# Attention into a gated mixture of experts: four steps' rows turned on VectorE instead of TensorE, two small products put later, and weight quarters asked for earlier

## The chip, the cores and the metric

One core of a Trainium2 chip runs the whole kernel in one launch. The metric is the device time of an execution in microseconds (us). Three runs of the kernel before gave 443.42, 445.30 and 445.82 us; the median is 445.3.

The core's engines are named as the profile names them: PE (TensorE matmuls) with PEld (its weight loads), DVE (VectorE), ACT (ScalarE), POOL (GpSimd) and SP (SyncE, which here only issues DMAs). Each engine takes its instructions in order, and each waits by semaphores for the others and for DMAs.

## What is computed

A linear attention with decay, block by block, whose output is the input of a mixture of experts. Each token goes to one of eight experts: the one with the largest logit, or, where a local gate says so, the expert of the token before.

```python
# attention: B=4, H=8, S=768, D=64; per head a decay lam and a state kv (D x D)
intra = (q_blk @ k_blk.T * Dmask) @ v_blk
inter = (q_blk * lam_pow) @ kv_state
out[block] = intra + inter
kv_state = lam_block * kv_state + (k_blk * rev_pow).T @ v_blk
# x = out of all heads, (4, 768, 512); E=8 experts, F=1024
logits = x @ w_gate
local_gate = sigmoid(x @ w_local)
e = argmax(logits[s]) if s == 0 or local_gate[s] < 0.5 else e_of_token_before
y[s] = softmax(logits[s])[e] * (relu(x[s] @ w1[e]) @ w2[e])
```

## The kernel before

**Two stages.** The attention runs in 24 steps. Step `s` handles one chunk of 128 tokens of one of the four sequences (`ORDER`: six chunks, four sequences each; `b = s % 4`, chunk `c = s // 4`). The experts' stage follows: tiles of 128 tokens that belong to one expert are gathered from `x_dram` by row numbers and go through that expert's two weight matrices. Its first tile is expert 0's, then more tiles with one expert each, then pairs of tiles and smaller parts. Each of PE, DVE, SP and POOL works in the order in which the program is written (`manual_schedule`); only ACT's order is the scheduler's.

**One step `s` of the attention**, in program order (the loop at the end of the step functions below):

- SP asks for the input of step `s+5` (`loaded`, 1 MB, 0.75 MB from step 20 on) into one of six buffers, which step `s-1` must have left.
- POOL scales query and key of step `s+3` (`prepare`: `qd` L178, `kd` L181).
- In the steps in `QUARTERS`, SP asks for a quarter (512 KB) of the first expert's `w1` into `w1t[0]` (L831).
- PE makes the scores of step `s+1` (`scores`, tile `ps`); DVE multiplies them with the mask (`sm`, L213, two instructions). For the steps in `WIDE`, the scores are eight products of whole 128x128 blocks (L201); for the others they are sixteen smaller ones that leave out a quarter of each block that the mask makes zero (L209).
- PE multiplies the state with `qd` (`from_state`, L236); ACT decays the state (L240).
- `logits`, then the extra work listed for `(s, 0)`, then every fourth step `gates` (L308).
- PE mixes values (`mix`, L249) and ACT copies the result to `xc` (L252), which holds one chunk per sequence and so is written again four steps later.
- PE makes the state's addition (`update`, L263), DVE adds it (`kv`, L266).
- The 128 rows of step `s-1` have to be turned (features to rows) and written to `x_dram`. There are two ways. `rows_of` does it with four PE products into `pk` (L273), an ACT copy to `xn` (L278) and a 256 KB write on ACT's queue (L282). `turned_rows` does it with one DVE instruction (L294), for the steps in `TURNED`, which says in which step it is done; the four steps of a chunk share one half of `w1t[1]` as their buffer, and after the last of them `group_out` writes all four with four DMAs of 256 KB on SP's queue (L302).
- The extra work listed for `(s, 1)`.

**The extra work** finds each token's expert while the attention still runs: `fresh_experts` (DVE only, ends with `mark` L425), `along_sequences` (PE products of the marks L433, then DVE `stay` L436 and a scan `run` L442), `experts_of` (PE products of the runs L449, then DVE `hot` L451), `ranks` (PE L460 and L461 on `hot`, ACT, DVE), `masks` (`lane`, L485), `first_tiles`, `tokens_to_first_tiles`, `brought`, `by_slots`, `chances`. The index 0 stands for chunks 0 and 1, index 1 for chunk 2. In step 20, `ahead` makes POOL gather the rows of the first two tiles (L725, `xg<-x_dram`); `prepare` of step 22 stands ahead of it in POOL's order, and `prepare` of step 23 behind it.

**The hand-over.** In step 23 PE turns the first gathered tile (`first_turned`, L734), DVE copies it (`xt`, L735), and the first expert's first product follows (`hidden`, L753). `w2` of the first expert is asked for in step 20 (L833), the second expert's weights in step 23 (L836, L837).

**Semaphores of the DMAs.** The DMAs of SP's and ACT's queues take eight semaphores in turn, in the order in which the scheduler places them; a DMA that takes a semaphore waits until the one that had it before has landed, and SP issues nothing else in the meantime.

Of the kernel before, what the change touches and what calls it, by code (L numbers as in the profile page):

```python
# [24 lines left out]
B, H, S, DH = 4, 8, 768, 64  # L25
# [12 lines left out]
NA = B * CA  # L38
PARTS = [(0, 8), (8, NA), (NA, NT)]
LOADS = 6  # L40
QUARTERS = [16, 17, 18, 19]
WIDE = [3, 4, 5, 7, 9, 11]
TURNED = {**{r: r + 1 for r in range(3 * B)}, 11: 13, 20: 22, 21: 23, 22: 23}
WARM = 10
KA = -(-(NA * P - E * (P - 1)) // P)

# [19 lines left out]
def kernel(  # L66
# [106 lines left out]
    def prepare(s):  # L173
        b, c = ORDER[s]
        x = inp[s]
        if c:
            qd = qds[s] = att.tile([P, A, P], F32, name="qd", bufs=3)
            nc.gpsimd.tensor_tensor(qd, x[:, 0].rearrange("p (a i) -> p a i", i=P), lamq, ALU.mult)  # L178
        if c + 1 < NC:
            kd = kds[s] = att.tile([P, DM], F32, name="kd", bufs=3)  # L180
            nc.gpsimd.tensor_tensor(kd.rearrange("p (h d) -> p h d", d=DH),  # L181
                                    x[:, 3].rearrange("p (h d) -> p h d", d=DH),
                                    rev.unsqueeze(2).broadcast_to([P, H, DH]), ALU.mult)
# [3 lines left out]
    def scores(s):  # L187
# [8 lines left out]

        if s in WIDE:
            for a in range(A):
                for u in range(2):
                    rows = slice(DH * u, DH * u + DH)  # L200
                    nc.tensor.matmul(ps[u][:, a], lhsT=kt[rows, a], rhs=qt[rows, a],  # L201
                                     start=True, stop=True, skip_group_check=True)
        for a in range(A if s not in WIDE else 0):
            for j in range(2):
# [92 lines left out]
    def group_out(k):  # L297

        n = sum(r // B == k for r in TURNED)
        rows = x_dram[B * P * k:B * P * k + n * P, :]  # L300
# [72 lines left out]
    def constants_6():  # L373
        for k in range(4):
            nc.scalar.copy(dupq[:, QP * k:QP * k + QP], ident[:, :QP])
        row = ints[0][:, 2 * P:2 * P + 1]
        nc.vector.tensor_scalar(row, row, P - QP, None, ALU.bitwise_and)
        nc.vector.tensor_scalar(fourth, row, 1.0 / QP, None, ALU.mult)
# [19 lines left out]
    def pool(i):  # L398
        return pools[i == 2]

    def hot_of(i):
        lo, hi = PARTS[i]
        return hots[lo // NA][:, :, lo % NA:lo % NA + hi - lo]

    def fresh_experts(i):

        lo, hi = PARTS[i]
        n = hi - lo
        lg = lt[:, lo:hi, :E]
        if not i:  # L410
            nc.vector.memset(lt[0:1, :B, E:], -1.0)
        if i == 2:
            room = rt.tile([P, 2, NA, E], F32, name="each0", bufs=1).rearrange("p k n e -> p (k n e)")
            mx, best, mark = (room[:, n * (E + k):n * (E + k) + n] for k in range(3))
            top, mark = room[:, :n * E].rearrange("p (n e) -> p n e", e=E), mark.bitcast(BF16)[:, :n]
        else:
            mx, best = (rt.tile([P, n], F32, name=f"{k}{i}", bufs=1) for k in ("mx", "best"))
            top = rt.tile([P, n, E], F32, name=f"top{i}", bufs=1)
            mark = rt.tile([P, n], BF16, name=f"mark{i}", bufs=1)
        nows["mx", i], nows["mark"] = mx, mark  # L420
        nc.vector.tensor_reduce(mx, lg, axis=AX.X, op=ALU.max)
        nc.vector.tensor_tensor(top, lg, mx.unsqueeze(2).broadcast_to([P, n, E]), ALU.is_equal)
        nc.vector.tensor_tensor(top, top, down.unsqueeze(1).broadcast_to([P, n, E]), ALU.mult)
        nc.vector.tensor_reduce(best, top, axis=AX.X, op=ALU.max)
        nc.vector.scalar_tensor_tensor(mark, lt[:, lo:hi, E], FRESH, best, ALU.is_le, ALU.mult)  # L425

    def along_sequences(i):

        lo, hi = PARTS[i]
        n = (hi - lo) // B  # L430
        prow = pr[:B, :P * n]
        for c in range(n):
            nc.tensor.matmul(prow[:, P * c:P * c + P], lhsT=nows["mark"][:, B * c:B * c + B], rhs=identb,  # L433
                             start=True, stop=True, skip_group_check=True)
        stay = pool(i).tile([B, P * n], BF16, name=f"stay{i}", bufs=1)
        nc.vector.tensor_scalar(stay, prow, 0.0, None, ALU.is_equal)  # L436
        run = runs[i] = pool(i).tile([B, P * n], BF16, name=f"run{i}", bufs=1)
        before = 0.0
        if i:
            before = rt.tile([B, 1], F32, name="carry", bufs=1)  # L440
            nc.scalar.copy(before, runs[i - 1][:, -1:])
        nc.vector.tensor_tensor_scan(run, stay, prow, before, ALU.mult, ALU.add)  # L442

    def experts_of(i):
        lo, hi = PARTS[i]
        n = hi - lo
        pe = pr[:, P * CA:P * CA + n]
        for c in range(n // B):
            nc.tensor.matmul(pe[:, B * c:B * c + B], lhsT=runs[i][:, P * c:P * c + P], rhs=identb[:B, :B],  # L449
                             start=True, stop=True, skip_group_check=True)  # L450
        nc.vector.tensor_tensor(hot_of(i), pe.unsqueeze(1).broadcast_to([P, E, n]),  # L451
                                down.unsqueeze(2).broadcast_to([P, E, n]), ALU.is_equal)

    def ranks(i):

        lo, hi = PARTS[i]
        n, hot = hi - lo, hot_of(i)
        ptot = pr[:, :E * n].rearrange("p (e t) -> p e t", e=E)
        prank = pr[:, E * NA:E * NA + E * n].rearrange("p (e t) -> p e t", e=E)
        nc.tensor.matmul(ptot, lhsT=onesb, rhs=hot, start=True, stop=True, skip_group_check=True)  # L460
        nc.tensor.matmul(prank, lhsT=beforeb, rhs=hot, start=True, stop=True, skip_group_check=True)  # L461
        tot = pool(i).tile([P, E, n + 1], F32, name=f"tot{i}", bufs=1)
        nc.scalar.copy(tot[:, :, 1:], ptot)
        if i:
            nc.scalar.copy(tot[:, :, 0:1], counts[i - 1])
        else:
            nc.vector.memset(tot[:, :, 0:1], 0.0)
        incl = pool(i).tile([P, E, n + 1], F32, name=f"incl{i}", bufs=1)
        nc.vector.tensor_tensor_scan(incl.rearrange("p e t -> p (e t)"), go[i].rearrange("p e t -> p (e t)"),
                                     tot.rearrange("p e t -> p (e t)"), 0.0, ALU.mult, ALU.add)  # L470
        counts[i] = incl[:, :, n:]
        where = pool(i).tile([P, E, n], F32, name=f"where{i}", bufs=1)
        nc.vector.tensor_tensor(where, prank, incl[:, :, :n], ALU.add)
        nc.vector.tensor_tensor(where, where, hot, ALU.mult)
        rank = pool(i).tile([P, n], I32, name=f"rank{i}", bufs=1)
        with nc.allow_low_precision("whole numbers"):
            nc.vector.tensor_reduce(rank, where.rearrange("p e t -> p t e"), axis=AX.X, op=ALU.add)
        nc.vector.tensor_scalar(place[:, 0, lo:hi], rank, P - 1, None, ALU.bitwise_and)
        nc.vector.tensor_scalar(place[:, 1, lo:hi], rank, -P, None, ALU.bitwise_and)

    def masks(i):

        lo, hi = PARTS[i]
        lane = onehots[i] = (act if i == 2 else route).tile([P, hi - lo, P], BF16, name=f"lane{i}", bufs=1)
        nc.vector.tensor_tensor(lane, countb.unsqueeze(1).broadcast_to([P, hi - lo, P]),  # L485
                                place[:, 0, lo:hi].unsqueeze(2).broadcast_to([P, hi - lo, P]), ALU.is_equal)
# [301 lines left out]
    def number(k, n):  # L788
# [2 lines left out]


    extras = {
        (6, 1): constants_2, (7, 1): constants_3, (8, 1): constants_4, (9, 1): constants_5, (10, 1): constants_6,
        (9, 0): lambda: fresh_experts(0), (10, 0): lambda: along_sequences(0), (11, 0): lambda: experts_of(0),
        (12, 0): lambda: ranks(0), (13, 0): lambda: fresh_experts(1), (14, 0): lambda: (along_sequences(1), masks(0)),
        (15, 0): lambda: experts_of(1), (16, 0): lambda: ranks(1), (17, 0): first_tiles,
        (18, 0): tokens_to_first_tiles, (19, 0): lambda: (brought(0, (0, 1)), masks(1)),
        (19, 1): lambda: by_slots(0, (0, 1)), (20, 0): lambda: (ahead(0, 0), ahead(1, 1), rows_out(0)),
        (20, 1): lambda: chances(0), (21, 0): lambda: chances(1), (22, 0): lambda: brought(0, (2, 3, 4)),  # L800
# [6 lines left out]
    with tc.manual_schedule(engines={PE, DVE, SP, POOL}):  # L807
# [16 lines left out]
        for s in range(NS):  # L824
            if s + LOADS - 1 < NS:
                loaded(s + LOADS - 1)
            if s + 4 < NS and s != 1:
                prepare(s + 3)
            if s in QUARTERS:
                j = QUARTERS.index(s)  # L830
                nc.sync.dma_start(out=w1t[0][:, j], in_=w1_src(0)[:, j])  # L831
# [29 lines left out]
            if s:  # L861
                update(s)
            if s > 1 and s - 1 not in TURNED:
                rows_of(s - 1)
            for r in [r for r in TURNED if TURNED[r] == s]:
                turned_rows(r)
                if r + 1 not in TURNED or r % B == B - 1:
                    group_out(r // B)
# [491 lines left out]
```

## Time and profile before

| | |
|---|---|
| median of three runs | 445.3 us |
| the profiled execution: its time, its span | 444.67 us, 442.9 us |
| granted TensorE clock in it, mean | 0.995 |
| busy: PE, PEld, DVE, ACT, POOL | 426.8, 354.4, 287.7, 194.9, 109.0 us |
| first product of the experts' stage (L753) | starts at 98.73 us |
| DMA: moved, mean rate | 124.84 MB, 282 GB/s |

All times inside an execution count from the first instruction of its span. The span is 1.8 us shorter than the execution's own time. The profile's views used here are the page (busy times, the span in 40 slices, the costliest groups), the chain of waits that ended last, the list of who waited for whom, the timeline of an engine, and windows (busy time of each engine, the granted clock, the share of time in which the 16 DMA engines were busy, and GB/s, for a stretch). In a timeline row the columns are start, length, engine, line, operation, output<-input, count, and in brackets the idle time before it with its releaser; rows of equal instructions are merged, and `SPq` and `ACTq` are DMA issues.

Steps of the attention as they lie in the trace, by the start of their scores on PE (the scores made in step `s` are those of step `s+1`):

| step | 13 | 14 | 15 | 16 | 17 | 18 | 19 | 20 | 21 | 22 |
|---|---|---|---|---|---|---|---|---|---|---|
| scores start, us | 55.30 | 59.23 | 63.76 | 67.20 | 71.69 | 75.62 | 80.16 | 84.82 | 89.50 | 93.20 |

### The profile page before, as it was taken

To read this page: it belongs to the slowest core of one execution; us is meant where nothing else is said; L and a number is where in the kernel's file an instruction comes from. 1 tells how busy PE (TensorE), PEld (TensorE's weight loads), DVE (VectorE), ACT (ScalarE), POOL (GpSimd) and SP (SyncE) were. 2 spreads that over 40 slices of the span, in tenths; PEclk is the share of its full clock that TensorE was granted. 3 is DMA by queue.
4 is the path that set the end of the run, shared out by engine and by line. 5 is a ranking of instruction groups with operands and counts; after the bars stand their busy time and mean duration, and the time that the engine had idled before them with its cause. 6 is when DMAs were issued, how large, how long until landed. Compare 5 with 4: busy or idle time off the path is not lost.

```text
span 442.9 us, 10337 instructions
## 1 busy us (share of the span) xinstructions
PE 426.8 (96%) x4094; PEld 354.4 (80%) x4094; DVE 287.7 (65%) x564; ACT 194.9 (44%) x592; POOL 109.0 (25%) x120
## 2 busy tenths in 40 slices
PE   6999899899999999999999999999999999999993
PEld 6788687677766786978777999667899999898982
DVE  5767997892239959857473785100587879878661
ACT  4245556336455105564234556451455454565110
POOL 4494584420100042205111302200202021020101
PEclk9999999999999999999999999999999999999998
DMA  7999999999999889999993799996164828370101
GB/s 262 410 366 366 361 350 323 348 341 342 347 395 392 294 304 396 399 396 404 394 398 136 255 400 367 343 368 210 40 215 146 314 81 300 128 269 3 55 1 52
DMA packets 48351, 124.84 MB, mean 282 GB/s; under 512 B 3164, under 2 KB 10844, under 8 KB 46368
## 3 DMA queue, kind: packets, MB, share of 16 engines
q1 hardware_dynamic: 42624, 108.03, 66.6%
q0 software_dynamic: 4368, 13.90, 8.9%
q10 hardware_dynamic: 1296, 2.10, 1.3%
q8 instruction: 36, 0.59, 0.5%
q14 instruction: 27, 0.22, 0.1%
HBM read 124.02 MB, written 12.91 MB: 309 GB/s over the span
## 4 chain that ended last, share of the span: by engine, by line
PE 75%; DVE 9%; DMA 8%; issue 6%; POOLq 0%; POOL 0%; ACT 0%; DVEq 0%
PE ps L753 13%; PE pk L759 12%; PE ps L983 12%; PE pk L988 11%; DMA out_dram<-y,sidxp 6%; PE po L983 5%; PE pl L988 4%; PE po L249 3%; DVE sm L213 3%; PE pr L1144 2%; PE pr L1122 2%; PE ps L209 2%; PE pk L263 1%; PE ps L201 1%; PE po L236 1%
## 5 line engine op out<-in xcount | busy, mean ns | idle before, releaser
L753 PEld LDWEIGHTS ps<-xt,w 128*128 128x128 f32 x512 | 58.2, 192 | 3.2 <-issue 2.3
L753 PE MATMUL ps<-xt,w 128*128 128x128 f32 x512 | 59.1, 276 | 0.5 <-DVE xt L735 0.5
L759 PE MATMUL pk<-w,h 128*128 128x512 f32 x128 | 56.6, 594 | 0.0
L759 PEld LDWEIGHTS pk<-w,h 128*128 128x128 f32 x128 | 23.7, 191 | 26.3 <-issue 25.5
L768 POOL DMA_INDIRECT out_dram<-y,sidx x14 | 14.0, 1001 | 105.4 <-DVE y L785 46.5
L725 POOL DMA_INDIRECT xg<-x_dram,gidx x25 | 25.8, 1033 | 56.4 <-DVE lg L739 34.1
L746 ACT COPY xp<-xlast 32x128 f32<-32x128 f32 x128 | 37.8, 296 | 1.7
L213 DVE TENSOR_TENSOR sm<-ps,mask 128x512 f32<-128x512 f32 x46 | 29.5, 681 | 7.8 <-PE ps L201 4.1
L785 DVE TENSOR_SCALAR y<-pk,gate 128x512 f32<-128x512 f32 x8 | 6.0, 744 | 43.9 <-PE pk L759 25.8
L746 ACT COPY xp<-lg 32x128 f32<-32x128 f32 x112 | 33.0, 295 | 2.6
L755 ACT ACTIVATE h<-ps 128x512 f32<-128x512 f32 x16 | 9.6, 597 | 55.2 <-PE ps L753 55.2
L178 POOL TENSOR_TENSOR qd<-inp,lamq 128x512 f32<-128x512 f32 x20 | 25.7, 1285 | 26.2 <-DMA inp<-in_qkv_dram 23.4
L983 PEld LDWEIGHTS ps<-xp,w 128*128 128x128 f32 x256 | 30.5, 192 | 1.6 <-issue 1.3
L983 PE MATMUL ps<-xp,w 128*128 128x128 f32 x256 | 31.3, 276 | 0.0
L983 PE MATMUL ps<-xs,s 128*128 128x128 f32 x256 | 31.2, 275 | 0.0
L988 PE MATMUL pk<-w,h 128*128 128x256 f32 x128 | 30.5, 381 | 0.0
L988 PE MATMUL pk<-s,hsum 128*128 128x256 f32 x128 | 30.3, 380 | 0.0
L249 PE MATMUL po<-sm,inp 128*64 128x128 f32 x384 | 27.9, 280 | 2.3 <-DVE sm L213 1.6
L983 PEld LDWEIGHTS ps<-xs,s 128*128 128x128 f32 x256 | 29.9, 192 | 0.0
L249 PEld LDWEIGHTS po<-sm,inp 128*64 128x64 f32 x384 | 21.0, 136 | 10.1 <-issue 5.8
L988 PEld LDWEIGHTS pk<-s,hsum 128*128 128x128 f32 x128 | 24.0, 190 | 3.2 <-DVE s L1071 0.2
L988 PEld LDWEIGHTS pk<-w,h 128*128 128x128 f32 x128 | 23.6, 191 | 3.3 <-issue 0.6
(282 smaller groups left out, 784.4 us busy)
## 6 DMA issues: line engine op xcount, KB each, us to landing
w<-in_w_dram SPq DMA_DIRECT2D x43, 2048.0 KB, 12.0
inp<-in_qkv_dram SPq DMA_DIRECT2D x15, 1024.0 KB, 10.8
inp<-in_qkv_dram SPq DMA_DIRECT2D x10, 512.0 KB, 8.4
x_dram<-w SPq DMA_DIRECT2D x12, 256.0 KB, 5.7
inp<-in_qkv_dram SPq DMA_DIRECT2D x4, 768.0 KB, 8.2
x_dram<-xn ACTq DMA_DIRECT2D x8, 256.0 KB, 6.8
w<-in_w_dram SPq DMA_DIRECT2D x4, 512.0 KB
x_dram<-inp SPq DMA_DIRECT2D x4, 192.0 KB, 7.8
```

The costliest lines, as they stand in the source:

```text
L178: nc.gpsimd.tensor_tensor(qd, x[:, 0].rearrange("p (a i) -> p a i", i=P), lamq, ALU.mult)
L209: nc.tensor.matmul(ps[u][half, a, first:], lhsT=kt[rows, a, half], rhs=qt[rows, a, first:], start=True, stop=True, skip_group_check=True)
L213: nc.vector.tensor_tensor(sm[:, u], ps[u], mask[:, u], ALU.mult)
L249: nc.tensor.matmul(head(a, u), lhsT=vn[:, a, u], rhs=sm[:, u, a], start=(not c and a < 2), stop=True, skip_group_check=True)
L725: nc.gpsimd.indirect_dma_start(out=xg, out_offset=None, in_=x_dram[:n, :], in_offset=bass.IndirectOffsetOnAxis(ap=gidx[i][:, j:j + 1], axi ...
L746: copy(xt[QP * j:QP * j + QP, :, QP * k:QP * k + QP], blocks[QP * k:QP * k + QP, :, j])
L753: nc.tensor.matmul(ph[:, j], lhsT=w1t[w][:, d, P * f:P * f + P], rhs=xtt[i][:, d], start=(d == 0), stop=(d == DT - 1))
L755: nc.scalar.activation(hq[half, i], ph, ACT.Relu)
L759: nc.tensor.matmul(pys[i], lhsT=hq[f // 4, i][:, f % 4], rhs=w2t[w][:, f], start=(f == 0), stop=(f == FT - 1))
L768: apart(nc.gpsimd.indirect_dma_start(out=out, out_offset=bass.IndirectOffsetOnAxis(ap=sidx[i][:, j:j + 1], axis=0), in_=y, in_offset=None, ...
L983: nc.tensor.matmul(to[:, m], lhsT=a[:, k, P * m:P * m + P], rhs=b[:, k], start=(new and not m and not k), stop=(k == 1), skip_group_check= ...
L988: nc.tensor.matmul(to, lhsT=a[:, f], rhs=b[:, f], start=(new and not f), stop=(f == FT // 2 - 1), skip_group_check=True)
```

## The change

Four tables of the kernel change; no function does.

- `TURNED`: the rows of steps 12 to 15 are turned by DVE. Rows 12, 13 and 14 are all turned in step 15, rows 15 in step 16, and `group_out(3)` writes the four in step 16, with four DMAs on SP's queue, behind the input of step 21 and ahead of the inputs of steps 22 and 23. Four times four PE products, an ACT copy and a write on ACT's queue go away. The buffer is the half of `w1t[1]` that chunk 1 used.
- `WIDE`: the scores of step 13 use the whole blocks.
- `QUARTERS`: the four quarters of `w1t[0]` are asked for in steps 12 to 15, that is, behind the inputs of steps 17, 18, 19 and 20 on SP's queue; before, it was in steps 16 to 19, behind the inputs of steps 21, 22 and 23.
- `extras`: `along_sequences(0)` and `experts_of(0)` move from the first place of steps 10 and 11 to their second, behind `mix` and `update`; `along_sequences(1)` and `experts_of(1)` do the same in steps 14 and 15, where `masks(0)` stays in the first place. `constants_6` stays where it was.

```diff
-QUARTERS = [16, 17, 18, 19]
-WIDE = [3, 4, 5, 7, 9, 11]
-TURNED = {**{r: r + 1 for r in range(3 * B)}, 11: 13, 20: 22, 21: 23, 22: 23}
+QUARTERS = [12, 13, 14, 15]
+WIDE = [3, 4, 5, 7, 9, 11, 13]
+TURNED = {**{r: r + 1 for r in range(4 * B)}, 11: 13, 12: 15, 13: 15, 20: 22, 21: 23, 22: 23}
...
     extras = {
-        (6, 1): constants_2, (7, 1): constants_3, (8, 1): constants_4, (9, 1): constants_5, (10, 1): constants_6,
-        (9, 0): lambda: fresh_experts(0), (10, 0): lambda: along_sequences(0), (11, 0): lambda: experts_of(0),
-        (12, 0): lambda: ranks(0), (13, 0): lambda: fresh_experts(1), (14, 0): lambda: (along_sequences(1), masks(0)),
-        (15, 0): lambda: experts_of(1), (16, 0): lambda: ranks(1), (17, 0): first_tiles,
+        (6, 1): constants_2, (7, 1): constants_3, (8, 1): constants_4, (9, 1): constants_5,
+        (9, 0): lambda: fresh_experts(0), (10, 1): lambda: (constants_6(), along_sequences(0)), (11, 1): lambda: experts_of(0),
+        (12, 0): lambda: ranks(0), (13, 0): lambda: fresh_experts(1), (14, 0): lambda: masks(0), (14, 1): lambda: along_sequences(1),
+        (15, 1): lambda: experts_of(1), (16, 0): lambda: ranks(1), (17, 0): first_tiles,
```

SP's DMAs of this stretch in program order, with the DMA whose semaphore each has to wait for where that is not long past (as the two built programs list them):

| before | after |
|---|---|
| input 17 | input 17, quarter 0 |
| input 18 | input 18, quarter 1 |
| group 2 (four) | group 2 (four) |
| input 19 | input 19, quarter 2 |
| input 20 | input 20, quarter 3 |
| input 21 | input 21 |
| quarter 0, behind row 14's write (ACT) | group 3, first, behind `turned_rows(15)` |
| input 22 | group 3, second, behind row 16's write (ACT) |
| quarter 1, behind row 15's write (ACT) | group 3, third and fourth, behind quarter 2 and input 20 |
| input 23 | input 22, behind input 21 |
| quarters 2 and 3, behind row 16's write and input 21 | input 23, behind group 3's first |
| `w2` of the first expert, behind quarter 0 | `w2` of the first expert, behind row 17's write (ACT) |

## The prediction

> **What bounds the kernel now.** First the chain of waits: from the first expert's product on it is PE alone.
>
> ```profile
> 97.49 0.61 DVE inp L294
> 98.10 0.59 DVE xt L735
> 98.73 3.84 PE ps L753 x32
> ```
>
> Columns: start, length, what. From 98.73 to 381 us the pieces are PE's, one on the other, and the page has PE busy for 426.8 of 442.9 us. The diff touches nothing there, so what it is worth is how far the start at 98.73 moves. It hangs on DVE's copy of the first gathered tile (L735).
>
> Next DVE's timeline. From 40.2 to 64.6 us its rows lie one on the other; then PE is late, and in steps 15 to 17 DVE idles 0.16 + 0.69 + 0.94 + 0.34 + 1.01 = 3.14 us, four of these gaps here:
>
> ```profile
> 66.81 0.42 DVE L266 TENSOR_TENSOR kv<-pk,kv 128x256 f32<-128x256 f32 x1 [0.69 <-PE pk L263]
> 68.17 1.29 DVE L213 TENSOR_TENSOR sm<-ps,mask 128x512 f32<-128x512 f32 x2 [0.94 <-PE ps L209]
> ...
> 71.22 0.42 DVE L266 TENSOR_TENSOR kv<-pk,kv 128x256 f32<-128x256 f32 x1 [0.34 <-PE pk L263]
> 72.66 1.29 DVE L213 TENSOR_TENSOR sm<-ps,mask 128x512 f32<-128x512 f32 x2 [1.01 <-PE ps L209]
> ```
>
> From 73 us on DVE is nearly full again, to 98.7. Third, the windows: the DMA engines are busy all the time (last two columns: their busy share, GB/s), and slow while a group's rows are written (62 to 68 us).
>
> ```profile
> 52.00:60.00 8.00, 8.00 (x194) 6.29 (x190) 7.44 (x19) 4.71 (x16) 5.57 (x5) 1.00 1.01 420
> 62.00:68.00 6.00, 6.00 (x157) 5.34 (x155) 4.34 (x9) 3.83 (x12) 5.12 (x4) 1.00 1.01 258
> 76.00:84.00 8.00, 6.94 (x162) 5.67 (x155) 7.66 (x24) 4.54 (x15) 2.75 (x3) 1.00 0.90 309
> 84.00:96.00 12.00, 10.98 (x221) 7.94 (x221) 10.04 (x37) 3.11 (x10) 4.96 (x4) 1.00 1.03 402
> ```
>
> Fourth, SP's and POOL's own waits and rows, for how input 22 and the first gather come:
>
> ```profile
> SPq L831 <- DMA x_dram<-xn: 11.1, 3, 8.2
> ```
> ```profile
> 76.97 0.99 SPq L171 DMA_DIRECT2D inp<-in_qkv_dram  x1
> ```
> ```profile
> 84.23 1.46 POOL L178 TENSOR_TENSOR qd<-inp,lamq 128x512 f32<-128x512 f32 x1 [3.99 <-DMA inp<-in_qkv_dram]
> 86.22 1.20 POOL L725 DMA_INDIRECT xg<-x_dram,gidx  x1 [0.52 <-DVE gidx L650]
> 87.72 1.01 POOL L725 DMA_INDIRECT xg<-x_dram,gidx  x1 [0.30 <-issue]
> ```
>
> SP stood 8.2 us behind a row's write; input 22, asked for at 76.97, landed at 84.1; POOL was waiting for it, and the gathers of the first two tiles stand behind that `qd`.
>
> **Part 1: rows 12 to 15 on DVE, step 13 wide.** PE loses four groups of L273, each 0.59 us from its start to the next one's (58.64 to 59.23), 2.36 us; the wide scores cost 43.97 - 42.88 = 1.09 us against 0.72 (55.30 to 56.02), +0.37. ACT loses four copies of 0.59 us, behind which nothing of the chain stands: 0. DVE gains four L294 of 0.63 us (46.58 - 45.95), 2.52 us, three of them in step 15 and one in 16, where the 3.14 us of idle time are. But PE, being faster, would have shortened that idle time, and the marks' second `hot` (L451) now stands behind three transposes, with PE's `ranks` product waiting for it. Lined up: DVE ends `lane` at 63.46, not 64.16 (`stay` and `run`, 0.70, now follow); `kv` 63.80, `stay` and `run` 64.50, `sm` 65.70, `kv` 66.05, three transposes 67.95, `hot` 68.10. PE, done with step 16's state product at 65.7 + 0.72 + 0.55 = 67.0, waits 1.1 us, then does `ranks` 0.15, gates 1.00, mix 0.93, update 0.56, scores 0.72: 71.5. DVE by then has done `sm` and ranks (70.5), `kv` (71.1), the last transpose (71.75), and its `sm` ends at 72.95; before, at 73.86. That is -0.9, less the wide scores (0.37), which PE does inside that line: -0.5, with bounds of -2.0 (all of DVE's larger idle times from 53 to 98 us, 4.55, filled up, less 2.52) and 0.
>
> **Part 2: products behind the update.** PE no longer stands 1.11 us at 44.64 for `mark`. DVE's order stays what it was but for three ops, and it is DVE that is full there: 0. The cover is DVE; in 40 to 64 us its windows hold 0.86 us of idle time, the most that can be had: -0.9 to 0.
>
> At one point DVE's cost is not its own: L539 took 1.22 us for 128x8, L541 beside it 0.17, and POOL's `qd` ran over exactly that time (76.39 to 77.66). The Trainium skill, "SBUF — State Buffer", section "Who interferes with whom", says that such a DVE operation and a GpSimd one exclude each other for a whole instruction; this trace agrees. By that rule a `qd` that falls elsewhere gives back or takes about 1 us; I give it no term.
>
> **Part 3: what now comes ahead of input 22.** Before, one quarter did; now all four, and group 3. Three quarters more are 1.57 MB, at 410 GB/s (between the 420 and 402 above) 3.8 us. Group 3 replaces four row writes of the same 1.05 MB: at the 258 GB/s of the window in which group 2 went 4.1 us, instead of 2.6 at 402: +1.5. The share of 0.90 in 76 to 84 us can be filled up: -0.8. So +4.5 us from bandwidth alone, 84.1 to 88.6.
>
> The skill speaks for less: "DMA: Bandwidth & Descriptors", "Specifications", has line rate from 512 B on, which is the length of a group's pieces (a row's 128 floats). By it the group would cost what rows cost, and input 22 come 1.5 us sooner; the window says 258 against 420 GB/s, and the sum keeps the window.
>
> **Part 4: the new wait on SP.** By the listing of the changed program, group 3's second DMA takes the semaphore of row 16's write on ACT's queue. Before, quarter 0 stood so behind row 14, the 8.2 us shown. Row 16's write was issued at 76.34 before; with part 1 at about 75.8. It lands 5.4 us later (row 16 before: quarter 2, which waited for it, went out at 81.74) to 8.6 (row 14: 67.93 to 76.54): 81.2 to 84.4. Behind it on SP are the rest of group 3, inputs 22 and 23 and the first expert's `w2`. What they take: before, group 2's second DMA went out at 61.65 and input 19, behind it, let POOL go at 73.91, 12.3 us. Now a fourth of the group is gone already (-1.0), the input is 0.25 MB smaller (-0.6), and one row's write in the way is fewer (-0.7): 10.0. Input 22 lands at 91.2 with the shorter wait, at 94.4 with the longer; by part 3 alone at 88.6. I take 91.2, since 5.4 us is what this same write took.
>
> Who waits for it. PE's scores of step 22 started at 89.50; but their `sm` had to wait for DVE until 91.86, so with 0.72 us of scores 91.1 is soon enough: 0 (3.3 at 94.4). POOL: 1.46 us of `qd`, then the first gather at about 92.8 instead of 86.22. The second of the two gathers landed 6.9 us after its issue (the page's median is 6.5; one at 96.85 landed at 100.25, 3.4): 99.7. PE turns the tile (0.65), then does step 23's state product (0.55) and mix (0.93), while DVE copies: first product at 101.8 instead of 98.73, **+3.1**. This is counted from SP's and ACT's rows, so part 1's 0.5 is in it (as 75.8) and is not taken off again. Bounds: input 22 at 88.6 and the quickest gather, 3.4 us, give 93.6, before the 95.92 at which PE turned to it: 0 here, and parts 1 and 2 remain; input 22 at 94.4 and 6.9 give 96.0 + 6.9 + 2.1 = 105.0, +6.3.
>
> The quarters themselves gain nothing: before, the last one landed by 92.06, where SP's next DMA waited for it, and it is used at 98.73. `w2` of the first expert goes out at about 86 behind row 17's write; the DMAs ahead of it (5.4 us of it included) end near 99, and PE needs it at 108.55: 0.
>
> **Sum.** +3.1 us for the first product, and all that follows moves with it. The profiled execution's 444.67 becomes 447.8; the median of the runs shown lies 0.6 above that execution, so **448.4**. The forecast's own range: 446.0 (a gather of 4.5 us instead of 6.9) to 451.
>
> **Rivals.**
> - *The load is covered.* Input 22 lands by 89, because row 16's write finds an emptier queue; the lead of 5.4 us (84.1 to 89.50) pays for it. For it: DMA has little left to do when SP stands still. Against: SP asks for nothing meanwhile, so the work comes later. Then part 1 remains: 445.3 - 0.5 = 444.8, no change.
> - *Faster.* The mechanism is DVE: its gaps take up the transposes and PE's shorter steps pull the rest ahead, up to the bounds of parts 1 and 2, -2.9, so 442.4. It decides if the first gather goes out by 88 us, thus if input 22 lands before 86. For it: 3.14 us of idle time just there. Against: all four quarters are ahead of that input.
> - *Worse than forecast.* Row 16's write takes 8.6 us, as row 14's did, and input 22 lands at 94.4: 445.3 + 6.3 = 451.6. For it: that was the wait which SP showed before. Against: row 14's write had a group's and two inputs' traffic ahead.
> - *The change does other than it says* is out: the listing has the four groups of L273 gone and four L294 more.
>
> **How the numbers follow.** A measurement of this kernel can tell about 0.5%, 2.2 us. Forecast 0.56, worse 0.15, covered 0.18, faster 0.11. Of the forecast's 0.56 its lower end, 446.0 to 447.5, gets 0.06, as one late load makes the next late too. Slower 0.50 + 0.15 = 0.65, same 0.06 + 0.18 = 0.24, faster 0.11. The range 444.2 to 451.2 leaves out the faster case and about half of the worse one.
>
> **What would show it.** Right: SP's row of group 3 split, the second DMA some 9 us behind the first; POOL idle for input 22 until past 90; PE idle at L734 for the gather; L753 starting near 102. Wrong: L753 starting at 98 or sooner, POOL's first gather at 87, or a stall elsewhere: in step 16 at L460 for more than 2 us, or in the experts' stage, where I expect none.

## The result, and the profile after

The changed kernel takes 448.60 us (median of 21 runs, 445.43 to 450.28); the kernel before, in runs of the same chip, 445.69 us (median of 21, 443.42 to 449.75). The ratio is 1.0077, with a 95% interval of 1.0059 to 1.0095: slower, by 2.9 us between the medians. The profiled execution of the changed kernel took 449.11 us, its span 447.3 us, against 444.67 and 442.9 before.

The chain of waits of the changed kernel, where it ends in the experts' stage (`...` stands for lines left out):

```profile
83.47 0.69 PE pk L263 x16
84.15 0.58 PE pk L273 x4
...
84.77 7.47 DMA inp<-in_qkv_dram
...
92.37 1.55 PE ps L209 x24
93.92 0.87 PE po L236 x16
94.79 1.06 PE pl L316 x4
...
96.25 1.49 DVE kd L498
...
100.68 0.68 DVE sm L213
...
101.76 0.61 DVE inp L294
102.37 0.59 DVE xt L735
103.00 3.84 PE ps L753 x32
```

The last three lines are those shown of before, 4.27 us later (103.00 for 98.73); after them PE has no gap, as before. New is the line at 84.77: a load, input 22, is in the chain, and behind it come step 22's scores and logits (L316), then DVE's `chances` (L498) and the scores' mask of step 23. The chain puts a product of PE (L273) ahead of that load, but what SP had only just ended, at 84.66, is group 3, as its own rows show.

SP's own wait for a row's write, in the list of who waited for whom (total, times, longest):

```profile
SPq L302 <- DMA x_dram<-xn: 7.3, 1, 7.3
```

And rows of the timeline of SP, ACT, POOL, PE and DVE in the same kernel, in this order (the second is from a view that starts at 80 us and so shows the last three DMAs of the first by themselves):

```profile
74.71 9.95 SPq L302 DMA_DIRECT2D x_dram<-w  x4
...
82.32 2.34 SPq L302 DMA_DIRECT2D x_dram<-w  x3
84.77 2.12 SPq L171 DMA_DIRECT2D inp<-in_qkv_dram  x2
...
78.17 0.33 ACTq L282 DMA_DIRECT2D x_dram<-xn  x1
...
92.40 1.27 POOL L178 TENSOR_TENSOR qd<-inp,lamq 128x512 f32<-128x512 f32 x1 [9.96 <-DMA inp<-in_qkv_dram]
...
92.37 1.56 PE L209 MATMUL ps<-inp 64*64 64x128 f32 x32 [2.55 <-DMA inp<-in_qkv_dram]
...
100.19 0.66 PE L734 MATMUL pr<-ident,xg 128*128 128x128 f32 x4
...
94.00 1.29 DVE L213 TENSOR_TENSOR sm<-ps,mask 128x512 f32<-128x512 f32 x2 [2.82 <-PE ps L209]
```

Group 3's four DMAs take from 74.71 to 84.66: the first goes out at 74.71, the second at 82.32, when row 16's write (issued by ACT at 78.17) has landed. Inputs 22 and 23 stand behind them. Input 22 lands at 92.2; POOL has been idle 9.96 us, PE 2.55 and DVE 2.82. PE turns the gathered tile (L734) without any idle time before it: the gather is not what it waits for.

The windows of the changed kernel, three of them over stretches that are shown of before, and the last over the end of SP's wait, show what a standing SP costs:

```profile
62.00:68.00 6.00, 5.12 (x126) 4.22 (x125) 5.86 (x11) 2.33 (x9) 5.42 (x4) 1.00 1.03 351
76.00:84.00 8.00, 7.69 (x194) 6.66 (x189) 7.62 (x23) 5.19 (x16) 2.77 (x3) 1.00 0.71 244
84.00:96.00 12.00, 8.84 (x153) 6.43 (x151) 7.46 (x28) 2.46 (x6) 3.13 (x3) 0.86 0.93 302
80.00:82.30 2.30, 2.30 (x66) 1.89 (x64) 2.20 (x6) 1.23 (x5) 1.14 (x1) 1.00 0.22 70
```

From 76 to 84 us the DMA engines were busy 0.71 of the time (0.90 before) and moved 244 GB/s (309 before). From 80 to 82.3 us, while SP still stands, they were busy 0.22 of the time: little is left for them to do. Input 22's bytes, which PE waits for later, are not yet asked for.

### The profile page after: what moved, and what is told of

Its sections match the earlier page's. It is cut to its first block, busy times and chain, and to the rows that moved or that the text cites. A ratio compares the mean times of both kernels' runs of the same rounds, so it can differ in the third digit from the quotient of the medians.

```text
span 447.3 us, 10293 instructions
## 1 busy us (share of the span) xinstructions
PE 428.5 (96%) x4062; PEld 355.4 (79%) x4062; DVE 289.4 (65%) x568; ACT 193.0 (43%) x588; POOL 109.2 (24%) x120
## 4 chain that ended last, share of the span: by engine, by line
PE 74%; DMA 11%; DVE 7%; issue 6%; POOLq 0%; POOL 0%; ACT 0%; DVEq 0%
PE ps L753 13%; PE pk L759 12%; PE ps L983 12%; PE pk L988 11%; DMA out_dram<-y,sidxp 6%; PE po L983 5%; PE pl L988 4%; DMA inp<-in_qkv_dram 3%; PE po L249 3%; DVE sm L213 2%; PE ps L209 2%; PE pr L1144 2%; PE pr L1122 2%; PE ps L201 1%; PE po L236 1%
## 5 line engine op out<-in xcount | busy, mean ns | idle before, releaser
L759 PEld LDWEIGHTS pk<-w,h 128*128 128x128 f32 x128 | 23.6, 190 | 26.3 <-issue 25.6
L755 ACT ACTIVATE h<-ps 128x512 f32<-128x512 f32 x16 | 9.6, 598 | 56.2 <-PE ps L753 56.2
L240 ACT ACTIVATE kv<-kv,lamq 128x64 f32<-128x64 f32 x64 | 17.3, 339 | 22.1 <-PE po L236 22.1
```

The lines of the kernel that those rows point to most:

```text
L240: nc.scalar.mul(kv[:, a], kv[:, a], lamq[:, a, P - 1:P])
L755: nc.scalar.activation(hq[half, i], ph, ACT.Relu)
L759: nc.tensor.matmul(pys[i], lhsT=hq[f // 4, i][:, f % 4], rhs=w2t[w][:, f], start=(f == 0), stop=(f == FT - 1))
```

## The experiments

Theory A is the forecast's: SP stands behind row 16's write, because group 3's second DMA takes that write's semaphore, and so input 22 is late. Its rivals: B, the traffic put ahead of input 22 (quarters and group 3) delays it; C, the new order on PE and DVE costs the time. Each kernel below was timed in five rounds against the kernel before on the same chip.

**The round of the semaphores.** One input is asked for in two DMAs, which moves the round of the eight semaphores on by one, for every DMA behind it. Nothing else differs from the changed kernel.

```diff
-        nc.sync.dma_start(out=inp[s][:, :n], in_=qkv[s][:, :n])
+        for j in range(0, n, 2 if s == 20 else n):
+            e = min(n, j + (2 if s == 20 else n))
+            nc.sync.dma_start(out=inp[s][:, j:e], in_=qkv[s][:, j:e])
```

> The changed kernel, with the input of step 20 asked for in two halves. The bytes, their order and the work of every engine stay; one DMA more moves the round of eight semaphores on by one, so that group 3's second DMA takes that of input 18 instead of that of row 16's write. Theory A (SP's wait behind row 16's write makes input 22 late): SP issues group 3 in one go from about 75, input 22 by 78 instead of 84.8, it lands by 88.6 at the latest (the forecast's figure for bandwidth alone), PE's scores of step 22 no longer wait for it, L753 starts near 99.5 to 100.5 instead of 103.0, the time is 445.5 to 446.5, so 2 to 3 us under the changed kernel. Theory B (the traffic put ahead of input 22, quarters and group 3, is what delays it): it still lands near 92 and the time stays at 448 to 449. Theory C (the loss comes from PE's and DVE's new order and the instruction stall in step 16): no change either, 448 to 449.

Measured: 445.65 us, ratio 1.0011 [0.9991, 1.0031]. No loss can be told any more, with the same bytes in the same order and the same work on every engine. Rows of its timeline, SP's, ACT's and then PE's (line numbers are two higher in this kernel: L304 is the group's write, L173 the input, L280 the row's copy, L284 its write, L736 the tile's turning, L755 the first product):

```profile
72.19 6.38 SPq L304 DMA_DIRECT2D x_dram<-w  x4
80.75 1.53 SPq L173 DMA_DIRECT2D inp<-in_qkv_dram  x2
...
79.00 0.59 ACT L280 COPY xn<-pk 128x512 f32<-128x512 f32 x1 [0.61 <-PE pk L275]
81.57 0.33 ACTq L284 DMA_DIRECT2D x_dram<-xn  x1
...
96.45 0.66 PE L736 MATMUL pr<-ident,xg 128*128 128x128 f32 x4 [1.34 <-DMA xg<-x_dram,gidx]
...
98.66 3.84 PE L755 MATMUL ps<-xt,w 128*128 128x128 f32 x32
```

Group 3 is out by 78.58 instead of 84.66, input 22 at 80.75 instead of 84.77 (the expectation's 78 was too early: the group's third and fourth DMA still wait for input 20's halves, and input 22 then 2.1 us for an earlier input), and the first product starts at 98.66. A is shown; B and C, which had 448 to 449 here, are refuted as main causes. Now the gather is what PE waits for, 1.34 us.

The extra DMA did not do away with the wait, though; it moved it to ACT. In this kernel row 17's write takes the semaphore that row 16's had (the trace shows one number for both): its copy was done at 79.59, but ACT could issue it only at 81.57, 2.0 us later, and did nothing in between. All five kernels with halves, this one and four below, have this wait (2.0 to 4.1 us); the changed kernel and the one with group 3 late do not have it.

**Group 3 out of the way.**

```diff
-                    group_out(r // B)
+                    if r // B != 3:
+                        group_out(r // B)
+            if s == 19:
+                group_out(3)
```

> The changed kernel with group 3's four writes asked for at the end of step 19, behind the inputs of steps 22 and 23, where nobody waits for them before the experts' stage. All bytes stay. Theory A (SP's wait): by the listing, input 22 stands behind nothing late and goes out near 72 to 74, input 23 now stands behind row 16's write and goes out near 81 to 83, lands by 88 to 90, and is needed at 93. So no wait in step 21, L753 at 98.5 to 100 instead of 103.0 and 445 to 446. Theory B (traffic): group 3's 1.05 MB no longer lies ahead of the two inputs, so it also gives 445 to 446; this run tells A and B together from C. Theory C (PE's and DVE's new order costs the time): 448 to 449.

Measured: 445.87 us, 1.0016 [0.9986, 1.0047]. The time is as A and B had it, but the first product is at 96.11, sooner than either said and 2.6 us sooner than in the kernel before; and then PE waits in the experts' stage (rows of the timeline, PE's and then SP's):

```profile
96.11 3.84 PE L753 MATMUL ps<-xt,w 128*128 128x128 f32 x32 [0.50 <-DVE xt L735]
...
116.09 9.01 PE L753 MATMUL ps<-xt,w 128*128 128x128 f32 x64 [3.03 <-DMA w<-in_w_dram]
...
100.02 0.08 SPq L702 DMA_DIRECT2D w<-in_w_dram  x1
100.27 0.41 SPq L836 DMA_DIRECT2D w<-in_w_dram  x1
```

The second expert's `w1` (L836) stands on SP behind a conditional load (L702) that waits for the first `w2` to land. It was asked for at 100.27 and let PE go 15.8 us later, 3.03 us too late; and those products took 9.01 us instead of 7.41, at a granted clock that fell to 0.56 from 119 to 121 us. In the kernel before, L836 went out at 99.16, and PE came to that expert at 115.61 without waiting, 16.45 us later. Had the load taken as long there, the kernel before had 0.6 us to spare; but in another run below (part 2's order as before) PE did not wait 14.5 us after the issue, so the margin differs between executions, from 0.6 to 1.9 us or more. Here the gain ahead of this second wait was lost at it.

**The gather ahead of input 22's work**, in the changed kernel and in the one with input 20 in halves:

```diff
-            if s + 4 < NS and s != 1:
+            if s + 4 < NS and s not in (1, 19):
                 prepare(s + 3)
...
-(20, 0): lambda: (ahead(0, 0), ahead(1, 1), rows_out(0)),
+(20, 0): lambda: (ahead(0, 0), ahead(1, 1), prepare(22), rows_out(0)),
```

> The changed kernel with the first two gathers ahead of step 22's qd and kd in POOL's order, so that they no longer wait for input 22, which is as late as ever. The forecast had the first gather's landing (99.7) as what sets the end. If so, they now go out near 87 and the time falls to where the scores' chain ends; by the changed kernel's trace PE turned to the tile at 100.19 without waiting, so the scores of step 22 and the DVE work behind them set the end: 448 to 449, no change.

Measured: 448.96 us, 1.0075 [1.0046, 1.0103]: no change from the changed kernel. In its profile PE has no stall without a releaser and a granted clock of 1.00 from 66 to 73 us, and SP stood 8.8 us for row 16's write, so the stall that the changed kernel's own profile has in step 16 is not needed for the loss. The first gather goes out at 84.24 instead of 93.83, and the first product starts at 102.91 all the same, because PE waits for input 22 (rows of PE's timeline):

```profile
92.69 1.56 PE L209 MATMUL ps<-inp 64*64 64x128 f32 x32 [5.47 <-DMA inp<-in_qkv_dram]
...
102.91 3.84 PE L753 MATMUL ps<-xt,w 128*128 128x128 f32 x32
```

The scores of step 22 set the end in the changed kernel; that the forecast had the gather there is refuted.

> The kernel of the run with input 20 in halves, with the first two gathers ahead of step 22's qd and kd in POOL's order. In that run PE stood idle 1.34 us for the first gathered tile (issued 88.04 behind that qd, landed 96.45). If the gather sets the end there, it now goes out as soon as its row numbers are ready, 86 to 87, and L753 comes up to 1.3 us sooner: 444.3 to 445.3. If the scores' chain is as late as the gather, or if the gather only waits longer in a full queue: no change, 445.5 to 446.

Measured: 445.32 us, 1.0004 [0.9982, 1.0026]; against the run with halves no difference that can be told. The gather went out at 85.44, PE no longer waited for it, and the first product started at 98.79, because the scores' chain was as late. It leads through ACT, which stood 3.0 us behind row 16's write:

```profile
76.47 6.22 DMA x_dram<-xn
...
82.71 0.02 ACTq L284
```

PE also had stalls without a releaser, of 1.16 us up to 61.78 and 0.48 us up to 80.13, and waited 1.38 us for DVE up to 92.66.

**The parts alone.** Quarters in steps 16 to 19 again, in the changed kernel:

```diff
-QUARTERS = [12, 13, 14, 15]
+QUARTERS = [16, 17, 18, 19]
```

> The changed kernel with the quarters in steps 16 to 19 again. By the listing, group 3 stands behind no late write of ACT's, and input 22 stands behind quarter 0, asked for just before group 3. Theory A: SP's wait is for quarter 0, which takes some 5 to 8 us from its issue near 72, so input 22 goes out at 78 to 80 and lands at 86 to 89: 445.5 to 447. Theory B: 1.05 MB less of quarters ahead of input 22 (only quarter 0 is left before it), 2.6 us at 400 GB/s, so it lands near 89.6 and the time is 446 to 446.5. Theory C: 448 to 449.

Measured: 449.30 us, 1.0084 [1.0055, 1.0112]. A's and B's figures miss, and C's is near by another cause. Input 22 went out at 80.82 and landed at 87.2, near A's figures and ahead of B's 89.6. But the first product was at 101.55, after a stall of PE without a releaser of 2.12 us up to 89.11 and a clock of 0.56 behind it. And SP stood 5.6 us for a row's write at input 23; the second expert's `w1`, asked for at 104.83, cost 1.54 us more.

The kernel before with only the rows moved:

```diff
-TURNED = {**{r: r + 1 for r in range(3 * B)}, 11: 13, 20: 22, 21: 23, 22: 23}
+TURNED = {**{r: r + 1 for r in range(4 * B)}, 11: 13, 12: 15, 13: 15, 20: 22, 21: 23, 22: 23}
```

> The kernel before with rows 12 to 15 turned on DVE and written as group 3, nothing else. Input 22 stands behind quarter 0 as in the run with the old quarters. Theory A: 445 to 447, as there. Theory B: group 3 costs 1.5 us more than the rows, and nothing else comes ahead of input 22: 85.6, no loss, 445 to 446. Theory C: three transposes in step 15 and one in 16 cost DVE 2.5 us where it has 3.1 us idle; if it is these that lose the time, 447.5 to 449.

Measured: 448.11 us, 1.0047 [1.0019, 1.0076]. In its profiled execution (450.50 us, 2.4 above the median) the first product is at 98.48, so up to there rows on DVE cost nothing; C's figure is met by another cause, as PE's timeline shows:

```profile
119.65 8.77 PE L753 MATMUL ps<-xt,w 128*128 128x128 f32 x64 [4.22 <-DMA w<-in_w_dram]
```

With group 3 ahead of them, quarters 1 to 3 go out at 78.12 to 89.15, the first `w2` behind them at 89.63 (86.93 in the changed kernel), and L836 at 104.84. SP issued nothing from 79.53 to 87.52, ahead of input 23, the place of the 5.6 us in the run before. Whether the quarters behind group 3 or that wait made `w2` late, these two runs do not separate.

The kernel before with only the quarters moved:

```diff
-QUARTERS = [16, 17, 18, 19]
+QUARTERS = [12, 13, 14, 15]
```

> The kernel before with the quarters in steps 12 to 15 and nothing else. By the listing, input 22 stands behind row 15's write on ACT's queue, issued near 71 to 72. Theory A: that write lands by 77 to 79, input 22 goes out at 77 to 79 and lands at 82 to 86, which is soon enough for its scores (89.5): 445 to 446, no change. Theory B: three quarters more ahead of input 22, 3.8 us, 84.1 becomes 87.9, soon enough by itself, so 445.5 to 446.5. Theory C: PE's and DVE's order is that of before: no change, 445.7.

Measured: 447.27 us, 1.0047 [1.0027, 1.0066], where all theories said no change. From its list of who waited for whom, SP's waits:

```profile
SPq L171 <- DMA x_dram<-xn: 8.4, 3, 7.0
SPq L302 <- DMA x_dram<-xn: 4.8, 1, 4.8
```

I had followed the listing for input 22 only. The quarters shift the round of semaphores here too: group 2's third DMA stood 4.8 us behind a row's write, and input 20 stood behind row 14's, from 69.28 (the issue before it) to 77.57. It is A's mechanism at another place: PE waited up to 2.44 us for inputs, and the first product is at 102.14.

Step 13's scores in sixteen products, and then part 2's order as before, each in the kernel with halves, where the semaphores fall alike:

```diff
-WIDE = [3, 4, 5, 7, 9, 11, 13]
+WIDE = [3, 4, 5, 7, 9, 11]
```

> The kernel with input 20 in halves, with step 13's scores in sixteen smaller products as before; the semaphores fall as in that run. The prediction has the wide scores at +0.37 us on PE. If PE sets the order there: 445.3; if it is covered: 445.7. If the instruction stalls of PE come and go with the number of instructions ahead of them (theory C's part), the time can move by 1 us either way.

Measured: 446.70 us, 1.0042 [1.0013, 1.0072], above all figures but the last. Against the run with halves (1.0011 [0.9991, 1.0031]) the intervals overlap. Its profile has one stall of PE without a releaser, of 1.84 us up to 61.15, the first gather at 89.65 and the first product at 99.76. Whether the wide scores gain anything stays open.

```diff
-        (10, 1): lambda: (constants_6(), along_sequences(0)), (11, 1): lambda: experts_of(0),
+        (10, 1): constants_6, (10, 0): lambda: along_sequences(0), (11, 0): lambda: experts_of(0),
...
-        (14, 0): lambda: masks(0), (14, 1): lambda: along_sequences(1), (15, 1): lambda: experts_of(1),
+        (14, 0): lambda: (along_sequences(1), masks(0)), (15, 0): lambda: experts_of(1),
```

> The kernel with input 20 in halves, with the products of marks and runs ahead of mix and update again, as in the kernel before; the semaphores fall as in that run. The prediction has part 2 at 0, with a bound of -0.9. If that holds: 445.5 to 446. If part 2 gained its bound: 446.5. If it cost time: 445.

Measured: 445.89 us, 1.0011 [0.9988, 1.0035], the ratio of the run with halves. Part 2 is worth nothing that these runs can tell.

**Towards a faster kernel.** Group 3 late, and the second expert's `w1` in step 20:

```diff
                 nc.sync.dma_start(out=w2t[0], in_=w2_src(0))
+                nc.sync.dma_start(out=w1t[1], in_=w1_src(1))
                 weights(0)
...
-                nc.sync.dma_start(out=w1t[1], in_=w1_src(1))
                 nc.sync.dma_start(out=w2t[1], in_=w2_src(1))
```

> The kernel of the run with group 3 late, with the second expert's w1 asked for in step 20, right behind the first expert's w2, instead of in step 23 behind the two conditional loads. In that run the first product started at 96.11 us, 2.6 before the kernel before, and PE then stood 3.03 us and lost 1.6 us more at 116 us for that w1, asked for at 100.27 because SP stood at a conditional load until the first w2 had landed. If that is all that gave the gain back: w1 goes out near 93 to 95, when group 3 has left the buffer, lands before 113, no stall, 445.2 - 3.0 - 1.6 = 440.6 us of span, and a median of 442.5 to 443.5, 0.5 to 0.7 per cent faster than before. If the DMA engines have no more to give there: the stall stays, 445 to 446, or the gathers come later by what the w1 takes (L753 near 98 to 100).

Measured: 444.81 us, 0.9979 [0.9954, 1.0004]: less than expected, and not to be told from no change. The stall at the second expert is gone, but a new one came at the first, in PE's timeline:

```profile
97.31 3.81 PE L753 MATMUL ps<-xt,w 128*128 128x128 f32 x32 [0.69 <-DMA w<-in_w_dram]
```

That `w1` had to wait until group 3 had left its buffer (issued at 95.68), and the conditional load of the first expert's `w1` (L701), on which the first product depends, stood behind it until 97.09.

> The control for it: the kernel before with that same w1 asked for in step 20. Its PE never waits for it, so if the gain of the other run is of rows, quarters and the free SP, this one stays at 445 to 446; if the earlier w1 is worth something by itself, it is faster by as much.

The same edit in the kernel before. Measured: 444.43 us, 0.9985 [0.9963, 1.0006]. So the two can't be told apart: what the rows on DVE add to the moved load is not shown.

The last run takes them together: halves, group 3 at the end of step 18, and that `w1` between the two conditional loads (the edits shown above are left out).

```diff
+            if s == 18:
+                group_out(3)
...
-    def weights(g):
+    def weights(g, between=lambda: None):
...
         nc.sync.dma_start(out=w1t[g % 2], in_=w1_src(e), cond=other, cond_hint=False)
+        between()
...
-                weights(0)
+                weights(0, lambda: nc.sync.dma_start(out=w1t[1], in_=w1_src(1)))
```

> What the other runs point to, in one kernel: the changed kernel with input 20 in halves (so that by the listing neither input 22 nor 23 stands behind a row's write), group 3 at the end of step 18 behind both inputs, and the second expert's w1 asked for in step 20 between the two conditional loads. In the run with the early w1 the first product waited 0.69 us for the conditional load, which stood behind that w1, and it in turn 9.7 us behind group 3; here that load stands ahead of it. If the waits on SP were what ate the gain of part 1: both inputs go out by 76, group 3 by 82, the second w1 by 95, L753 starts at 95.5 to 96.6, no stall at 113, and the time is 442.5 to 443.5, 0.5 to 0.7 per cent faster than before. If the DMA engines are simply full, the gathers or that w1 come later by as much as the rest comes earlier, and it is 444.5 to 445.5.

Measured: 445.79 us, 1.0014 [0.9986, 1.0042], a miss. The loads did what was expected of them (inputs 22 and 23 at 71.77 and 76.00, group 3 by 82.99, the second `w1` at 89.98, no stall at that expert), and PE came later anyway. From the chain of waits:

```profile
60.92 1.81 issue
...
67.35 0.80 issue
...
74.24 0.57 issue
```

"Issue" is time in which PE waited for nothing that the profile shows; the three make 3.2 us. The other part is ACT's wait. Row 17's copy was done at 80.47, and ACT could issue its write, behind row 16's, only 4.1 us later; DVE then waited for ACT (rows of ACT's and DVE's timeline; L242 is the state's decay, L268 the state's addition):

```profile
84.53 0.33 ACTq L284 DMA_DIRECT2D x_dram<-xn  x1
84.90 1.06 ACT L242 ACTIVATE kv<-kv,lamq 128x64 f32<-128x64 f32 x4 [4.43 <-PE pr L643]
...
86.00 0.42 DVE L268 TENSOR_TENSOR kv<-pk,kv 128x256 f32<-128x256 f32 x1 [1.46 <-ACT kv L242]
```

Against the run with group 3 late, PE was 2.2 us behind at step 21's scores (84.78 for 82.60) and their mask, behind that wait, 3.2 us (86.82 for 83.64); the first product is at 99.69. No kernel here is shown to beat the one before.

## Why the prediction was right

448.4 us was forecast, 448.6 measured, and the main step, part 4, is shown by the run with halves. That the two numbers lie so close is luck: as a change, 3.1 us was forecast for the first product, and it was 2.9 us between the medians but 4.3 us for the first product of the profiled execution, where another path than the forecast's ended last. Point by point:

- **What bounds the kernel.** Right for the two kernels: nothing moved behind the first product. It was not seen how little the experts' stage of before has to spare at the second expert's `w1` (0.6 to 1.9 us or more, by the runs above).
- **Part 1, -0.5.** About right, but without effect. In a profile where PE has no stall without a releaser at all (group late), step 18's `sm` starts at 71.94 instead of 72.66, and PE's wait for `hot` at L460, forecast at 1.1 us, is 1.08; with two ahead of it, of 0.88 and 0.51 us (halves), it starts at 72.09. In the changed kernel's own profile `sm` starts at 74.60, behind a stall of 1.18 us and products at half clock. Later the gain grows: step 21's `sm` starts at 83.64 (group late) and 84.84 (halves) instead of 86.53.
- **Part 2, 0.** Right, as far as these runs can tell.
- **Part 3, +4.5 us from bandwidth.** Not decisive: with SP free, PE did not wait for input 22. Whether the quarters gain anything in company with the rows stays open.
- **Part 4, the wait.** Right in place and cause. Its two terms were off in opposite directions: row 16's write went out at 78.17 rather than 75.8, behind PE's stall and half clock, and took 4.1 us rather than 5.4, so SP was free at 82.32 (forecast 81.2). With the gather ahead and no stall they were 76.39 and 5.6 us, and SP was free at 82.03. What stood behind it took 9.9 us (forecast 10.0); input 22 landed at 92.2 (91.2).
- **Who waits for it.** This step failed. The forecast judged step 22's scores to have time until 91.1, put 0 on them and let the gather end the chain (+6.9 to 99.7), though its own 91.2 for the input was already 0.1 past that limit. Its sign for this, PE idle at L734 for the gather, did not come. The input came 1.1 us past the limit, and the scores' side then lost more than its lateness: 2.55 us of idle PE, products at half clock behind it (L209 1.56 us for 0.90), and `chances` (L498) stretched to 1.56 us (L503, of the same shape, takes 0.18) until POOL's `qd` of step 23 had ended. It came to 103.0; the gather, by the run that takes it off that path, did not matter. The two ends lay close together (101.8 forecast for the gather's, 103.0 measured for the scores'), which is why the sum held.
- **The rule on DVE and GpSimd.** The forecast gave it no term. L539 fell from 1.22 to 0.17 us, and L541 and L550 rose from 0.17 to 1.13 and 1.15, each beside a `qd` of POOL, as the rule of the Trainium skill's "SBUF — State Buffer", "Who interferes with whom", has it. In the chain of waits are L550's, ahead of input 22, whose time SP's wait set, and L498's, behind it.

## What to carry to other kernels

A DMA added or moved on a queue changes which earlier transfer every later one has to wait for. Before pricing its bytes, list for each DMA behind it whose semaphore it takes and when that one lands, in every step and not only the one of interest: here one wait of 7.3 us on SP was worth some 3 us of time, and one more DMA moved it to ACT's queue, where it was shorter and the loss could no longer be told. And look for the next wait behind the gain, with its margin: 2.6 us gained ahead of the second expert's load brought nothing.

## What the runs showed that was not expected

**PE's stalls without a releaser lie whole blocks of 256 instructions apart.** In 13 of the 14 profiles they lie at the same places of its program, or there are none, counted in PE's instructions from the start (products, weight loads and semaphore waits; stalls over 0.25 us). Seven of them:

```
kernel          stall in us @ instruction number, from 30 to 103 us
before          0.72@2242  0.48@3266
after           1.17@2498
halves          0.88@2242  0.51@2498  0.29@2754  1.08@3010
rows alone      0.89@1730  1.15@1986  1.47@2242  1.57@2754  1.12@3266
old quarters    0.75@1218  0.61@2242  0.29@2754  0.65@3010  2.12@3266
all together    0.64@1730  1.81@2242  0.80@2498  0.57@2754  0.65@3010
group late      none
```

To within one, all numbers are 194 more than a multiple of 256. The exception is the run with part 2's order as before, with 0.47 us at 3530. The list of DMA queues on the changed kernel's page (packets, MB, share of the 16 engines' span) has two of the kind "instruction":

```profile
q8 instruction: 36, 0.59, 0.5%
q14 instruction: 27, 0.22, 0.1%
```

0.59 MB in 36 packets are 16.4 KB each. The Trainium skill, "Runtime: NRT & Kernel Launch", "Instruction fetch mechanics", has just these blocks of 256 instructions and 16 KiB and calls the cost of crossing one mostly hidden; here the stalls made between nothing and 6.2 us from 30 to 103 us of one execution. That the fetch waits in the crowd of other transfers is an inference: no run changed it alone.

**Behind some short gaps PE's clock was halved.** Behind the stall of 1.18 us the changed kernel's granted clock (third number from the end, in the windows) was

```profile
68.50:72.00 3.50, 3.44 (x33) 1.48 (x33) 2.57 (x8) 1.14 (x5) 0.00 (x0) 0.51 0.95 339
```

and behind the 2.55 us up to 92.37 again 0.50, from 92.5 to 95.8 us. Length alone does not decide: it was 0.50 behind 1.34 us too (step 13's scores in sixteen products, from 94.2 us), and stayed at 1.00 behind 1.81 us (at 60.92 in the last run) and 2.44 us (quarters alone, up to 83.28). The skill's "TensorE: Matmul & The Clock Gate", "Why this matters for your kernels", asks for no idle gaps above about 3 us; the trace agrees with its half rate and differs in the gap that is enough.
